# Blocks of 384 tokens in row groups of 128, a second product that yields rows, and a reciprocal held in PSUM, in an attention and two-mixture kernel

## The chip, the cores and the metric

The kernel runs on one NeuronCore of a Trainium2 chip. The metric is the device time in microseconds of one execution, as the median of several runs. Five engines work from queues of their own and meet through semaphores: PE (matrix products, results in PSUM), DVE and ACT (elementwise work, both reach SBUF and PSUM), POOL (elementwise work in SBUF and indirect DMAs) and SP (here it only issues DMAs).

## The reference

```python
# q, k, v: batch 8, heads 8, 576 tokens, head width 64
k_p = k.reshape(B, H, 72, 8, D).mean(axis=3)       # and v_p alike: 72 averaged keys
attn = softmax(q @ k_p.T / 8)                      # over the 72 keys
x = (attn @ v_p) as rows                           # 4608 tokens x 512
h = x @ w_in                                       # 512 x 2048, float64 in DRAM
g = (a0 + a1*h + a2*h*h + a3*h**3) / (1 + |b0|*|h| + |b1|*h*h + 1e-6)
y = g @ w_out                                      # 2048 x 512, float64 in DRAM
logits = y @ w_gate                                # 8 experts, the best one of each token
out = gate * (relu(y @ w1[e]) @ w2[e])             # 512 x 1024 x 512, float32
```

## The kernel before

Products are made in float32r from a high and a low part of each operand, so a product of two matrices is three products (high by high, high by low, low by high).

**Head.** `w_in` and `w_out` are turned from float64 into a high and a low float32r part, in 40 pieces (`conv_magnitude` on ACT, `conv_bits` and `conv_join` on DVE, `conv_high` on ACT, `conv_low` on POOL; line 281 `tick` does one stage of each for a different piece). 34 of the 40 ticks stand ahead of the first product, woven into the attention of the first block; the others stand in the first steps of the loop. The head ends with the first product at 109.4 us.

**Block loop.** A block is half a batch: 288 tokens, in three row groups of 96. It takes 16 steps, one for each chunk of 128 of the hidden width, so there are 16 blocks and 256 steps. Step t has, in this order of the code:

- `mm1(t)`: 12 products of 128x128 by 128x288, the hidden values of the chunk, by chunk on the partitions and token on the columns, into PSUM (`hps`, two buffers).
- `act_c(t - 2)`: Ln and Exp on ACT give the reciprocal of the denominator in SBUF (`Bt`), then two operations on DVE (lines 509 and 510) and later a third (512) finish the quotient with one step of Newton's.
- `act_d(t - 3)`: the quotient is split, the high part by ACT (518), the low part by POOL (519).
- `act_a(t)`, `act_b(t)`: numerator and denominator from `hps`, with ACT (484, 492, 499), DVE (493, 497) and POOL (500).
- `mm2(t - 4)`: 12 products of 128x128 by 128x288; the weights are the stationary operand, so the result `y` has the 512 output columns on the partitions, in four PSUM tiles, and the tokens on the columns.

`LAG`, here 4, is how many steps `mm2` is behind `mm1`. The attention of the next block is cut into events at points, two points to a step (`EVENTS`); one unit, a pair of heads of one block, takes 8 points, which is four steps. When a block is done, `evac` copies `y` to SBUF, `route1` and `route2` find expert and place of each token, and `rows` turns `y` back into rows with PE and writes them to DRAM (`yd`). Keys and values are pooled once for a batch, but the split of the values is made anew in each of its two blocks (`at_v`).

**Second mixture.** 17 full slots of 256 tokens and four half ones of one expert each: lists and rows are fetched by indirect DMAs, the expert's weights are loaded (512 KB pieces), split by ACT and DVE, and multiplied. The first three slots are known early and run while the last blocks are routed.

Nothing is scheduled by a planner: each engine takes its instructions in the order in which the code issues them.

Of the kernel before, what the change touches and what calls it, by code (L numbers as in the profile page):

```python
# [33 lines left out]
BUSY = 17      # slots of the full size that always run  # L34


def feasible(nt):
# [10 lines left out]
def const_layout(nt, nb):  # L48
    """Columns of the array of shape constants."""
    nth, nf, nr = nt // SL, BUSY - EARLY, n_rest(nt)  # L50
    cols, o = {}, 0
    for name, w in (("ident", 128), ("val", E), ("base", E), ("thr", 2 * nth), ("item", nf + nr + NU + nr),
                    ("place", nf + nr + NU + nr), ("low", E * E), ("eid", E), ("tok", nb * 6), ("mask", 2), ("vmask", 2)):
        cols[name] = (o, w)
        o += w
# [3 lines left out]
def constants(nt, nb):  # L59
# [19 lines left out]
    b, r = np.divmod(np.arange(nb * 6), 6)  # L79
    put("tok", b[None] * 576 + 6 * p[:, None] + r[None])  # L80
# [6 lines left out]
def tile_kernel(  # L87
# [24 lines left out]
    R = 3  # L112
    N = R * G
    NBLK = 2 * B
    LATE = 6
    ROW = DM + 1
    # the first units spare VectorE, which the weights hold
    LAG, WHOLE = 4, 4
# [8 lines left out]
    t3p = ctx.enter_context(tc.tile_pool(name="t3p", bufs=3))  # L127
    ysp = ctx.enter_context(tc.tile_pool(name="ysp", bufs=2))
# [5 lines left out]
    elp = ctx.enter_context(tc.tile_pool(name="elp", bufs=3))  # L134
    first = ExitStack()
    o1 = first.enter_context(tc.tile_pool(name="o1", bufs=1))
    kvl = first.enter_context(tc.tile_pool(name="kvl", bufs=4))
    t2p = first.enter_context(tc.tile_pool(name="t2p", bufs=2))
# [17 lines left out]
    ones = one.tile([G, 128], BF16, name="ones")  # L156
# [20 lines left out]
    tok = one.tile([G, 6 * B], I32, name="tok")  # L177
    nc.vector.tensor_copy(tok, con("tok")[:G])

# [8 lines left out]
    def clear_rows():  # L188
        zero = ysp.tile([G, ROW], F32, tag="ys", name="zero")
        nc.gpsimd.memset(zero, 0.0)  # L190
        nc.sync.dma_start(yd[(B - 1) * S:, :].rearrange("(p r) c -> p r c", r=2 * R),
                          zero.unsqueeze(1).to_broadcast([G, 2 * R, ROW]))
# [4 lines left out]
    def rest_parts(dtype, rows):  # L197
        t = [o1.tile([rows, w], dtype, tag=f"rest{w}", name=f"rest{w}") for w in (128, N)]
        for x in t:
            nc.vector.memset(f32(x), 0.0)  # L200
        return t

    tail = rest_parts(F32, KB)
# [16 lines left out]
    def conv_load(c):  # L220
        j, i, o, w = PIECES[c]
        if c == 0:
            sr = wp.tile([128, 4, 512], I64, tag="w", name="sr")
            mr = wp.tile([128, 8, 512], F32, tag="w", name="mr")
            cv["ring"] = [sr[:, x] for x in range(4)], [mr[:, x] for x in range(8)]
        if j < RING:
            s, m = cv["ring"][0][c % 4], cv["ring"][1][c % 8]
        else:
            s = kvl.tile([128, 256], I64, tag="kv", name="s64")
            m = None  # L230
# [7 lines left out]
        cv[c] = [s, m]  # L238

    def words(c):  # L240
        """The upper words of a piece, and its quarters."""
        s = cv[c][0]
        return s.bitcast(U32).rearrange("p (n t) -> p n t", t=2)[:, :, 1], s.bitcast(U16).rearrange("p (n t) -> p n t", t=4)

    def conv_magnitude(c):
        """The upper word of a float64, read as a float32 without its sign, times 2^-112: the
        exponent's upper bits are 0, and three places further on it is float32's."""
        if cv[c][1] is None:
            cv[c][1] = kvl.tile([128, 256], F32, tag="cm", name="m64", bufs=3)
# [785 lines left out]
```

## Time and profile before

| | us |
|---|---|
| median of 3 runs (1734.96 to 1739.96) | 1739.53 |
| span of the profiled execution, first to last instruction | 1722.4 |
| head, to the first product | 109.4 |
| block loop, to the first back product of the second mixture | 1133.6 |
| second mixture, to the last output DMA | 462.6 |
| what follows it in the span | 16.8 |
| busy in the span: PE / DVE / ACT / POOL | 1530.5 / 1464.8 / 1158.1 / 906.7 |

The profiled execution has a span of 1722.4 us; its own time outside of the span isn't recorded, and the median of the runs is 17.1 us above it. The shares over the whole span hide the stages: the loop and the second mixture have different limits, so the table is by stage. PE's busy time counts a modelled end of each product, so a product that nothing follows at once looks longer than the interval to the next in a dense row.

### The profile page before, as it was taken

How to read it: one execution, taken by the hardware profiler on the slowest of the kernel's cores; microseconds unless marked ns; L12 is line 12 of the kernel's file. 1: busy time of each engine (PE TensorE's matmuls, PEld its weight loads, DVE VectorE, ACT ScalarE, POOL GpSimd, SP SyncE). 2: the span in 40 equal slices, each digit the busy share in tenths (PEclk: the TensorE clock that was granted, in tenths of full speed). 3: DMA queues.
4: the chain of work that ended last, by engine and by line, in shares of the span. 5: the costliest groups of instructions: out<-in, count | busy, mean ns of one | idle time of the engine just before them, and what ended most of it. 6: DMA issues, size and time to landing. Idle time of an engine off the chain costs nothing. (4 is left out here: it accounts for less than half of the span.)

```text
span 1722.4 us, 31453 instructions
## 1 busy us (share of the span) xinstructions
PE 1530.5 (89%) x10920; PEld 1446.9 (84%) x10920; DVE 1464.8 (85%) x2986; ACT 1158.1 (67%) x2668; POOL 906.7 (53%) x1035
## 2 busy tenths in 40 slices
PE   0368999899999799989999989999879999999995
PEld 0248898898999799889899989999879998999994
DVE  7999999999999799999999999998866656666661
ACT  3467777777778578778677867877645556565651
POOL 6958756855856665675685676555412112112120
PEclk9998999999999899999999999999989999999998
DMA  6622211101201311110120120003667777777760
GB/s 202 191 86 59 50 35 32 43 21 44 49 8 44 40 26 42 32 39 18 44 49 13 48 46 15 19 13 71 175 154 248 237 231 240 246 237 246 239 202 18
DMA packets 144932, 165.72 MB, mean 96 GB/s; under 512 B 54206, under 2 KB 97470, under 8 KB 144768
## 3 DMA queue, kind: packets, MB, share of 16 engines
q1 hardware_dynamic: 137152, 144.21, 29.8%
q0 software_dynamic: 7616, 19.45, 3.4%
q8 instruction: 88, 1.44, 0.5%
q14 instruction: 76, 0.62, 0.2%
HBM read 143.37 MB, written 20.77 MB: 95 GB/s over the span
## 5 line engine op out<-in xcount | busy, mean ns | idle before, releaser
L530 PE MATMUL y<-hi,wt 128*128 128x288 f32 x2048 | 480.5, 309 | 25.1 <-DVE yT L542 25.1
L477 PE MATMUL hps<-xT,wt 128*128 128x288 f32 x3072 | 469.4, 302 | 7.6 <-DVE C L497 6.9
L477 PEld LDWEIGHTS hps<-xT,wt 128*128 128x128 f32 x3072 | 426.1, 191 | 13.8 <-DVE C L497 13.4
L530 PEld LDWEIGHTS y<-hi,wt 128*128 128x128 f32 x2048 | 351.1, 192 | 28.4 <-DVE yT L542 28.4
L519 POOL TENSOR_TENSOR lo<-C,hi 128x288 fp32r<-128x288 f32 x256 | 236.0, 922 | 212.8 <-ACT hi L518 148.4
L530 PE MATMUL y<-lo,wt 128*128 128x288 f32 x1024 | 309.3, 302 | 25.9 <-POOL lo L519 25.9
L814 DVE TENSOR_TENSOR wt<-ws,wt 128x1024 fp32r<-128x1024 f32 x168 | 203.2, 1222 | 100.2 <-ACT wt L809 99.3
L500 POOL TENSOR_TENSOR A<-A,B 128x288 f32<-128x288 f32 x256 | 235.2, 919 | 85.6 <-ACT B L499 65.4
L510 DVE SCALAR_TENSOR_TENSOR A<-A,qone,B 128x288 f32<-128x288 f32 x256 | 233.3, 911 | 0.0
L823 PEld LDWEIGHTS h2ps<-x2T,wt 128*128 128x128 f32 x1632 | 214.4, 192 | 20.7 <-DVE lo L836 9.4
L823 PE MATMUL h2ps<-x2T,wt 128*128 128x256 f32 x1632 | 219.0, 284 | 9.1 <-DVE lo L836 8.9
L518 ACT ACTIVATE hi<-C 128x288 fp32r<-128x288 f32 x256 | 112.2, 438 | 168.0 <-DVE C L512 166.3
L856 PE MATMUL o<-wt,hi 128*128 128x512 f32 x608 | 220.9, 405 | 1.3 <-ACT yT L540 0.8
L530 PEld LDWEIGHTS y<-lo,wt 128*128 128x128 f32 x1024 | 198.0, 193 | 28.2 <-POOL lo L519 28.0
L809 ACT ACTIVATE wt<-ws 128x1024 fp32r<-128x1024 f32 x168 | 174.8, 1055 | 16.5 <-PE o L856 16.5
L509 DVE SCALAR_TENSOR_TENSOR C<-C,ab,B 128x288 f32<-128x288 f32 x256 | 157.1, 614 | 20.6 <-ACT B L508 20.4
L499 ACT ACTIVATE B<-A,ab 128x288 f32<-128x288 f32 x256 | 160.0, 625 | 0.0
L512 DVE SCALAR_TENSOR_TENSOR C<-A,C 128x288 f32<-128x288 f32 x256 | 156.6, 612 | 0.1
L507 ACT ACTIVATE B<-A,qone 128x288 f32<-128x288 f32 x256 | 136.2, 532 | 22.5 <-POOL A L500 21.2
L492 ACT ACTIVATE C<-hps,ab 128x288 f32<-128x288 f32 x256 | 150.0, 586 | 1.2 <-POOL lo L519 1.2
L835 ACT ACTIVATE hi<-h2ps 128x256 fp32r<-128x256 f32 x136 | 52.0, 383 | 142.4 <-PE h2ps L823 140.2
L856 PEld LDWEIGHTS o<-wt,hi 128*128 128x128 f32 x608 | 115.0, 189 | 22.0 <-ACT yT L540 1.1
(277 smaller groups left out, 2684.6 us busy)
## 6 DMA issues: line engine op xcount, KB each, us to landing
ws<-in_moe_w_dram SPq DMA_DIRECT2D x168, 512.0 KB
yd<-ys SPq DMA_DIRECT2D x48, 192.4 KB
kt<-in_k_dram SPq DMA_DIRECT2D x64, 144.0 KB
qt<-in_q_dram SPq DMA_DIRECT2D x128, 72.0 KB
sr<-in_moe_w_in_dram SPq DMA_DIRECT2D x12, 512.0 KB
sr<-in_moe_w_out_dram SPq DMA_DIRECT2D x12, 512.0 KB
vt<-in_v_dram SPq DMA_DIRECT2D x32, 144.0 KB
vt<-in_v_dram SPq DMA_DIRECT2D x32, 112.0 KB
```

The source lines that it names most:

```text
L477: nc.tensor.matmul(hps, lhsT=w_in_part(t, wi, kk, fl), rhs=xT[n, kk][:, xi, :], start=(i == 0), stop=(i == last))
L499: nc.scalar.activation(Bt, A, AF.Identity, scale=b1, bias=b0)
L500: nc.gpsimd.tensor_tensor(out=A, in0=A, in1=Bt, op=ALU.mult)
L509: nc.vector.scalar_tensor_tensor(out=C, in0=C, scalar=a0, in1=Bt, op0=ALU.add, op1=ALU.mult)
L510: nc.vector.scalar_tensor_tensor(out=A, in0=A, scalar=qone, in1=Bt, op0=ALU.add, op1=ALU.mult)
L512: nc.vector.scalar_tensor_tensor(out=C, in0=A, scalar=-2.0, in1=C, op0=ALU.add, op1=ALU.mult)
L519: nc.gpsimd.tensor_tensor(out=lo, in0=C, in1=f32(hi), op=ALU.subtract)
L530: nc.tensor.matmul(yps[n][d], lhsT=w_out_part(w, wi, fl)[:, d * 128:d * 128 + 128], rhs=g[gi], start=(fc == 0 and i == 0), stop=(fc == NFC ...
L809: nc.scalar.activation(s["wt"][j][:, 2 * i, :], s["ld"][c], AF.Copy)
L814: nc.vector.tensor_tensor(out=t[:, 2 * i + 1, :], in0=w, in1=f32(t[:, 2 * i, :]), op=ALU.subtract)
L823: nc.tensor.matmul(hps, lhsT=a_, rhs=b_, start=(i == 0), stop=(i == 3 * KD - 1))
L856: nc.tensor.matmul(s["o"][j], lhsT=hl[gi][:, x * 128:(x + 1) * 128], rhs=w_out_part(wt_, wi, fl), start=(first_ and n_ == 0), stop=(last_ ...
```

## The change

Blocks become 384 tokens, two thirds of a batch, in three row groups of 128. Two batches make three blocks, so the middle block of each three has tokens of two batches (`pieces_of`), and there are 12 blocks and 192 steps. 576 is no multiple of 128, so one row group in nine is put together from two batches, 64 and 64 rows.

```diff
-G = 96         # tokens of one row group
+G = 128
+R = 3
...
+    pair, i = divmod(t, PER2)
+    a, whole = 2 * pair, HEADROWS // G
+    tail = SEQ - HEADROWS
+    if i < whole:
+        return [(0, G, a, i, whole)]
+    if i == whole:
+        return [(0, tail, a, HEADROWS, 1), (tail, G, a + 1, 0, 1)]
+    return [(0, G, a + 1, tail + i - whole - 1, whole)]
...
-    LAG, WHOLE = 4, 4
+    LAG = 3
...
-    t3p = ctx.enter_context(tc.tile_pool(name="t3p", bufs=3))
-    ysp = ctx.enter_context(tc.tile_pool(name="ysp", bufs=2))
+    t3p = ctx.enter_context(tc.tile_pool(name="t3p", bufs=2))
+    ysp = ctx.enter_context(tc.tile_pool(name="ysp", bufs=3))
...
     def conv_magnitude(c):
...
+        w = PIECES[c][3]
+        cv[c][1] = py.tile([128, 512], F32, tag=f"y{c % 3}", name="mag")[:, :w]
+        nc.scalar.activation(cv[c][1], words(c)[1].bitcast(F32), AF.Abs, scale=2.0 ** -112)
...
-        nc.gpsimd.tensor_tensor(out=wt[j][:, 2 * i + 1, o:o + w], in0=cv.pop(c)[1],
-                                in1=f32(wt[j][:, 2 * i, o:o + w]), op=ALU.subtract)
...
+        (nc.gpsimd if j < RING else nc.vector).tensor_tensor(
+            out=wt[j][:, 2 * i + 1, o:o + w], in0=cv.pop(c)[2], in1=f32(wt[j][:, 2 * i, o:o + w]), op=ALU.subtract)
...
+        parts = [kvp.tile([128, 2, D], F32R, tag=f"va{j}", name=f"va{j}") for j in range(2)]
+        nc.scalar.activation(parts[0], va, AF.Copy)
+        nc.gpsimd.tensor_tensor(out=parts[1], in0=va, in1=f32(parts[0]), op=ALU.subtract)
+        kv_t[bb, hp][1:] = [[x.rearrange("j h d -> j (h d)") for x in parts], end]
...
+            A, C = el[t]
+            Q = py.tile([128, N], F32, tag="y3", name="Q")
+            nc.scalar.activation(Q, A, AF.Ln, bias=qone)
+            nc.scalar.activation(Q, Q, AF.Exp, scale=-1.0)
+            nc.vector.scalar_tensor_tensor(out=C, in0=C, scalar=a0, in1=Q, op0=ALU.add, op1=ALU.mult)
+            nc.vector.scalar_tensor_tensor(out=Q, in0=A, scalar=qone, in1=Q, op0=ALU.add, op1=ALU.mult)
+            el[t] = Q, C
...
+            yps[n] = [py.tile([G, DM], F32, tag=f"y{r}", name=f"y{r}") for r in range(R)]
...
+        for r in range(R):
+            for i, (wi, gi) in enumerate(((0, 0), (1, 0), (0, 1))):
+                nc.tensor.matmul(yps[n][r], lhsT=g[gi][:, r * G:(r + 1) * G], rhs=w_out_part(w, wi, fl),
+                                 start=(fc == 0 and i == 0), stop=(fc == NFC - 1 and i == 2))
...
+    def evac(n):
+        rows_t[n] = []
+        for r in range(R):
+            ys = ysp.tile([G, DM], F32, tag="ys", name="ys")
...
+            for lo, hi, dst in places(n * R + r):
+                nc.sync.dma_start(dst[:, :DM], ys[lo:hi])
...
-    P0, PACE, HEAD = 8, 1.55, 34      # the weights that are made ready before the first product
+    P0, PACE, HEAD = 6, 1.2, 39
...
-            p2["stg"] = ctx.enter_context(tc.tile_pool(name="stg", bufs=5))
+            p2["stg"] = ctx.enter_context(tc.tile_pool(name="stg", bufs=4))
...
-            act_c(t - 2, 0)
-        if 3 <= t < total + 3:
-            act_d(t - 3)
+            act_d(t - 2)
+        if 1 <= t < total + 1:
+            act_c(t - 1, 0)
```

In `mm2` the quotient is now the stationary operand and the weights move: 9 products of 128x128 by 128x512, whose result has tokens on the partitions. `evac` copies these rows and writes them to `yd` at once; for the routing each row group is turned by PE (`logits`), copied, and multiplied by `w_gate` (`logits2`). The gates follow in DMAs of one column (`gates`). The split values of a pair of heads are made once for a batch and kept. `y` needs three PSUM tiles instead of four; the fourth holds the reciprocal `Q`. 39 ticks instead of 34 stand ahead of the first product, and the quotient is finished one step earlier (`act_c(t - 1)`, `act_d(t - 2)`).

The order of the engines' instructions, in the middle of the loop, before and after. First **DVE**, one step and the start of the next. `C` is the numerator and then the quotient, `A` the denominator, `B` (now `Q`) the reciprocal, `hps` the hidden values in PSUM; equal numbers are the same tile.

```order
L509 SCALAR_TENSOR_TENSOR C_6547<-C_6547,ab_111,B_6552 128x288
L510 SCALAR_TENSOR_TENSOR A_6539<-A_6539,qone_116,B_6552 128x288
L493 TENSOR_TENSOR C_6669<-C_6669,hps_6640 128x288
L512 SCALAR_TENSOR_TENSOR C_6547<-A_6539,C_6547 128x288
L497 SCALAR_TENSOR_TENSOR C_6669<-C_6669,ab_111,hps_6640 128x288
```

The same place in the changed kernel:

```order
L555 SCALAR_TENSOR_TENSOR C_4850<-C_4850,ab_111,Q_4886 128x384
L556 SCALAR_TENSOR_TENSOR Q_4886<-A_4844,qone_116,Q_4886 128x384
L538 TENSOR_TENSOR C_4899<-C_4899,hps_4869 128x384
L560 SCALAR_TENSOR_TENSOR C_4850<-Q_4886,C_4850 128x384
L542 SCALAR_TENSOR_TENSOR C_4899<-C_4899,ab_111,hps_4869 128x384
```

The five operations keep their order; `Q` stands in PSUM where `B` and the product in `A` stood in SBUF, and the quotient that is finished belongs to the step just before instead of the one before that.

Then **ACT**, from the Ln of one step to that of the next. `hi` is the high part of the quotient; L507 and L508, now L553 and L554, are Ln and Exp.

```order
L507 ACTIVATE B_7583<-A_7566,qone_116 128x288
L508 ACTIVATE B_7583<-B_7583 128x288
L518 ACTIVATE hi_7695<-C_7513 128x288
L484 ACTIVATE A_7699<-hps_7678 128x288
L361 ACTIVATE qT_7705<-qps_7701 128x288
L492 ACTIVATE C_7715<-hps_7678,ab_111 128x288
L499 ACTIVATE B_7720<-A_7699,ab_111 128x288
L445 ACTIVATE xT_7740<-ops_7735 128x288
L507 ACTIVATE B_7657<-A_7636,qone_116 128x288
```

The changed kernel, from the last operation of a step to the last of the next:

```order
L544 ACTIVATE Bt_5597<-A_5569,ab_111 128x384
L566 ACTIVATE hi_5628<-C_5512 128x384
L553 ACTIVATE Q_5632<-A_5569,qone_116 128x384
L554 ACTIVATE Q_5632<-Q_5632 128x384
L529 ACTIVATE A_5637<-hps_5615 128x384
L410 ACTIVATE qT_5643<-qps_5639 128x384
L537 ACTIVATE C_5653<-hps_5615,ab_111 128x384
L544 ACTIVATE Bt_5658<-A_5637,ab_111 128x384
```

Before, Ln takes an `A` from two steps back (7566; the step's own is 7699). Now Ln takes the `A` (5569) that belongs to the L544 two rows above it, with POOL's product of the two in between, and `hi` moved ahead of Ln.

Last **PE**, the first product of a step and the start of its second. `pps` and `sps` are parts of the attention of the next block, `y` the result of the block.

```order
L477 MATMUL hps<-xT,wt 128x288 x12
L398 MATMUL pps<-cst,pt 16x96 x3
L530 MATMUL y_5039<-hi,wt 128x288
L530 MATMUL y_5039<-lo,wt 128x288
L530 MATMUL y_5039<-hi,wt 128x288
L530 MATMUL y_5040<-hi,wt 128x288
```

The changed kernel, with the outputs of a unit (`ops`) between:

```order
L419 MATMUL sps<-kbd,qT 128x144 x3
L522 MATMUL hps<-xT,wt 128x384 x12
L489 MATMUL ops<-pT_4920,va_3871 128x384
L489 MATMUL ops<-pT_4921,va_3871 128x384
L489 MATMUL ops<-pT_4920,va_3872 128x384
L489 MATMUL ops<-tail,end_132 128x384
L578 MATMUL y_4112<-wt,hi 128x512 x2
L578 MATMUL y_4112<-wt,lo 128x512
L578 MATMUL y_4113<-wt,hi 128x512 x2
```

In each step 24 products of 288 columns became 12 of 384 and 9 of 512, and the first of the low part moved from second to third in `mm2`.

## Rows read from the trace of the kernel before

**Rows 1.** Windows: stretch, length, busy us of PE, PEld, DVE, ACT, POOL; clock.

```profile
0.00:109.40 109.40, 31.03 (x105) 19.37 (x105) 96.95 (x145) 45.01 (x93) 81.93 (x69) 1.00 0.56 174
109.40:1243.00 1133.60, 1048.15 (x7905) 1018.86 (x7903) 1084.46 (x2368) 853.09 (x2139) 733.74 (x888) 0.98 0.18 41
1243.00:1705.60 462.60, 451.27 (x2914) 408.69 (x2914) 283.38 (x475) 260.01 (x438) 90.35 (x78) 0.99 0.69 216
1705.60:1722.40 16.80, 0.00 (x0) 0.00 (x0) 0.00 (x0) 0.00 (x0) 0.65 (x1) 0.54 0.03 11
```

**Rows 2.** DVE by line, 300 to 1100 us: busy us, mean ns, idle before.

```profile
L510 DVE SCALAR_TENSOR_TENSOR A<-A,qone,B 128x288 f32<-128x288 f32 x181 | 166.5, 920 | 0.0
L512 DVE SCALAR_TENSOR_TENSOR C<-A,C 128x288 f32<-128x288 f32 x182 | 111.0, 610 | 0.0
L509 DVE SCALAR_TENSOR_TENSOR C<-C,ab,B 128x288 f32<-128x288 f32 x182 | 108.9, 598 | 18.2 <-ACT B L508 18.1
L497 DVE SCALAR_TENSOR_TENSOR C<-C,ab,hps 128x288 f32<-128x288 f32 x182 | 91.4, 502 | 0.0
L493 DVE TENSOR_TENSOR C<-C,hps 128x288 f32<-128x288 f32 x182 | 79.6, 437 | 0.7
L331 DVE TENSOR_REDUCE kp<-kt 72x64 f32<-72x512 f32 x45 | 48.3, 1073 | 0.7
...
L374 DVE TENSOR_TENSOR pt<-sps,mx 96x432 f32<-96x432 f32 x46 | 27.8, 604 | 1.6
```

**Rows 3.** A line's instructions, 300 to 1100 us: duration ns min/median/max.

```profile
L497 DVE SCALAR_TENSOR_TENSOR C<-C,ab,hps x182: 495/502/510, 300.5 to 1099.0; 128x288 f32<-128x288 f32 x182
...
L510 DVE SCALAR_TENSOR_TENSOR A<-A,qone,B x181: 500/1057/1936, 303.0 to 1096.6; 128x288 f32<-128x288 f32 x181
```

**Rows 4.** Timeline of DVE and POOL at one place: start, length.

```profile
505.82 1.23 DVE L510 SCALAR_TENSOR_TENSOR A<-A,qone,B 128x288 f32<-128x288 f32 x1
505.90 0.82 POOL L519 TENSOR_TENSOR lo<-C,hi 128x288 fp32r<-128x288 f32 x1
```

**Rows 5.** POOL, the same view.

```profile
L500 POOL TENSOR_TENSOR A<-A,B 128x288 f32<-128x288 f32 x183 | 168.2, 919 | 55.9 <-ACT B L499 42.7 <-PE y L530 7.8
```

**Rows 6.** PE timeline in the block loop: start, length, count.

```profile
501.07 1.75 PE L477 MATMUL hps<-xT,wt 128*128 128x288 f32 x12
502.65 0.41 PE L359 MATMUL qps<-cst,qt 96*128 96x96 f32 x3
...
509.15 0.98 PE L368 MATMUL sps<-kbd,qT 128*96 128x144 f32 x6
```

**Rows 7.** PE timeline in the second mixture.

```profile
1503.03 0.39 PE L856 MATMUL o<-wt,hi 128*128 128x512 f32 x1
...
1504.42 1.59 PE L823 MATMUL h2ps<-x2T,wt 128*128 128x256 f32 x12
```

**Rows 8.** PE, by line and shape, 300 to 1100 us.

```profile
L552 PE MATMUL tps<-wg,yT 128*96 128x8 f32 x264 | 23.4, 227 | 0.0
```

**Rows 9.** ACT by line, 300 to 1100 us, columns as in group 2.

```profile
L507 ACT ACTIVATE B<-A,qone 128x288 f32<-128x288 f32 x182 | 96.9, 532 | 22.2 <-POOL A L500 21.2
L508 ACT ACTIVATE B<-B 128x288 f32<-128x288 f32 x182 | 81.0, 445 | 5.8
L518 ACT ACTIVATE hi<-C 128x288 fp32r<-128x288 f32 x182 | 79.8, 438 | 121.0 <-DVE C L512 120.5
...
L616 ACT ACTIVATE ys<-rp 96x512 f32<-96x512 f32 x36 | 21.1, 587 | 0.0
```

**Rows 10.** DVE by line and shape, 0 to 109.4 us.

```profile
L257 DVE TENSOR_SCALAR sr<-sr 128x512 uint16<-128x512 uint16 x24 | 28.6, 1191 | 0.0
...
L262 DVE SCALAR_TENSOR_TENSOR mr<-mr,sr 128x512 uint32<-128x512 uint32 x24 | 21.0, 875 | 0.2
```

**Rows 11.** PE timeline where routing ends.

```profile
1283.55 2.93 PE L823 MATMUL h2ps<-x2T,wt 128*128 128x256 f32 x12 [8.94 <-DVE lo L836]
```

**Rows 12.** Waits, 1180 to 1320 us: total, times, longest.

```profile
ACT ys L616 <- DMA yd<-ys: 9.4, 1, 9.4
```

More of the change, by code (lines that the diff above doesn't have):

```diff
@@ L24 @@
 SL = 256
-G = 96
+G = 128
+R = 3
+HEADROWS = 512
 POOL = 8
@@ L78, in constants @@
     put("eid", np.arange(E))
-    b, r = np.divmod(np.arange(nb * 6), 6)
-    put("tok", b[None] * 576 + 6 * p[:, None] + r[None])
+    tok = np.zeros((128, nt // G))
+    for t in range(nt // G):
+        for lo, hi, batch, start, step in pieces_of(t):
+            tok[lo:hi, t] = batch * SEQ + start + step * np.arange(hi - lo)
+    put("tok", tok)
     put("mask", np.stack([p < 64, p >= 64], 1))
@@ L188, in clear_rows @@
     def clear_rows():
-        zero = ysp.tile([G, ROW], F32, tag="ys", name="zero")
+        zero = ysp.tile([96, ROW], F32, tag="ys", name="zero")
         nc.gpsimd.memset(zero, 0.0)
-        nc.sync.dma_start(yd[(B - 1) * S:, :].rearrange("(p r) c -> p r c", r=2 * R),
-                          zero.unsqueeze(1).to_broadcast([G, 2 * R, ROW]))
+        nc.sync.dma_start(yd[(B - 1) * S:, :].rearrange("(p r) c -> p r c", p=96),
+                          zero.unsqueeze(1).to_broadcast([96, S // 96, ROW]))
     KB = 2 * KP - 128
[L197 to L203, printed above, removed]
+    tail = o1.tile([64 + KB, N], F32R, name="tail")
+    nc.vector.memset(f32(tail), 0.0)
+    ends = [o1.tile([64 + KB, 128], F32R, name=f"end{i}") for i in range(HP + 1)]
+    for x in ends:
+        nc.gpsimd.memset(f32(x), 0.0)
     wt, cv = {}, {}
@@ L222, in conv_load @@
         if c == 0:
[L223 to L230, printed above, removed]
+            cv["ring"] = []
+            for x in range(2):
+                ring = wp.tile([128, 4, 512], I64, tag="w", name="sr")
+                cv["ring"] += [ring[:, y] for y in range(4)]
+        s = cv["ring"][c % 8] if j < RING else ysp.tile([128, 256], I64, tag="ys", name="s64")
         if i == 0:
@@ L298, in unit, with runs @@
         n, hp = divmod(U, HP)
-        return n, hp, *divmod(n, 2)
+        a, m = 2 * (n // 3), n % 3
+        return n, hp, a, (a, a + 1, None)[m]
+    def runs(n):
+        out_ = []
+        for r in range(R):
+            for lo, hi, batch, _, _ in pieces_of(n * R + r):
+                if out_ and out_[-1][2] == batch:
+                    out_[-1][1] = r * G + hi
+                else:
+                    out_.append([r * G + lo, r * G + hi, batch])
+        return out_
     def at_load_kv(U, h):
-        n, hp, bb, half = unit(U)
-        if half == 0:
+        n, hp, _, bb = unit(U)
+        if bb is not None:
             kt = kvl.tile([128, POOL * D], F32, tag="kv", name="kt")
@@ L342, in at_kT @@
     def at_kT(U):
-        n, hp, bb, half = unit(U)
-        if half == 0:
-            kp = kv_t[hp][0]
+        n, hp, _, bb = unit(U)
+        if bb is not None:
+            kp = kv_t[bb, hp][0]
             kps = pm.tile([128, KP], F32, tag="m", name="kps")
@@ L397, in at_pT @@
         for r in range(R):
[L398 removed]
+            nc.tensor.transpose(pps[:, r, :], pt[:, r, 128:] if h else pt[:, r, :128], ident)
         pps = pps.rearrange("j r g -> j (r g)")
         if h == 0:
[L401 removed]
+            parts = [o1.tile([128, N], F32R, tag=f"pT{j}", name=f"pT{j}") for j in range(2)]
@@ new lines, in tile_kernel, with places @@
+    rows_t, lg_t = {}, {}
+    def evac(n):
+        rows_t[n] = []
+        for r in range(R):
+            ys = ysp.tile([G, DM], F32, tag="ys", name="ys")
+            if r == 1:
+                nc.vector.tensor_copy(ys, yps[n][r])
+            else:
+                nc.scalar.activation(ys, yps[n][r], AF.Copy)
+            rows_t[n].append(ys)
+            for lo, hi, dst in places(n * R + r):
+                nc.sync.dma_start(dst[:, :DM], ys[lo:hi])
+    def places(t):
+        out_ = []
+        for lo, hi, batch, start, step in pieces_of(t):
+            at = batch * S + start
+            if step > 1:
+                first_ = start if batch % 2 == 0 else start - (SEQ - HEADROWS)
+                rows_ = yd[at - first_:at - first_ + step * G, :].rearrange("(p r) c -> p r c", r=step)[:, first_, :]
+            else:
+                rows_ = yd[at:at + hi - lo, :]
+            out_.append((lo, hi, rows_))
+        return out_
@@ L595, in route2 @@
         if n == NBLK - 3:
-            soon = early_tables()
-            for i in range(5):
-                agenda.setdefault(p + 2 + 2 * i, []).append((lambda: next(soon, None), None))
+            agenda.setdefault(p + 2, []).append((lambda: list(early_tables()), None))
         for r in range(R):
@@ L625, in after_block @@
             todo += [(p + 4, lambda _: next(tables, None))] * LATE
-        at, gap = {NBLK - 2: (p + 9, 3), NBLK - 1: (p + 5, 3)}.get(n, (p + 4, 1))
-        todo += [(at + gap * r, lambda _, r=r: rows(n, r)) for r in range(R)]
         return todo
@@ L995, in tile_kernel @@
                 evac(n)
-                extra += after_block(n, 2 * t + LEAD + (4 if n < NBLK - 2 else 3))
+                extra += after_block(n, 2 * t + LEAD + 2)
         main.back(g)
```

248 lines of the change are left out of this document (124 added, 124 removed).

## The prediction

> **What bounds the kernel now.** I read the windows by stage first, since the shares over the span mix stages with different limits. In the block loop DVE is busy for 1084.5 of 1133.6 us, 96%, and PE, by its modelled ends, for 1048.2, 92%; ACT has 75% and POOL 65% [rows 1]. Over 256 steps that is 4.43 us a step, of which DVE works 4.24. In the second mixture PE is busy for 451 of 462.6 us and nothing else is near it. In the head DVE is busy for 97 of 109.4 us. So DVE sets the pace of head and loop, PE that of the rest.
>
> Next I asked what fills DVE in the loop. The list of its instructions by line shows five operations of every step, 920, 610, 598, 502 and 437 ns on 288 columns, 3.07 us together [rows 2]. The two that read `hps` in PSUM keep their length: 495 to 510 ns for one line. The three that read two tiles in SBUF don't: the same work takes 500 to 1936 ns, in the median 1057 [rows 3]. The timeline shows when: one of them took 1.23 us beside a POOL product of 0.82 us that began with it [rows 4]. POOL makes two such products a step, 919 ns in the mean [rows 5]. So some 0.7 us of DVE's step (920, 610 and 598 down to about 500, 440 and 500) is waiting for POOL.
>
> **The change, part by part.**
>
> *Reciprocal in PSUM.* The three slow operations keep one operand in SBUF; the other, and in one case the result, moves to PSUM. The nearest row for that is the 502 ns line with its 495 to 510 [rows 3]. It shows no wait for POOL and no extra for the PSUM operand either, since the SBUF form has the same 500 ns when alone. I take those lengths; the bound on the other side is that nothing gets shorter. [...]
>
> *384 columns.* From 288 to 432 columns a DVE operation goes from 437 to 604 ns [rows 2], about 1.1 ns a column, so 96 more columns cost 0.1 us and the fixed part is paid 192 times, not 256. The five come to 500+500+440+502+437 = 2.38 us plus 0.53 for columns, 2.9 a step; neighbours overlap by some 0.05 each, which leaves 2.65. DVE's other work is now 4.24 - 3.07 + 0.25 = 1.4 us a step, 363 us in all; 48 units instead of 64, with a third more columns in part of their operations, and the split of the values made half as often and partly by POOL, leave some 80%, 290 us or 1.5 a step. DVE: 4.15 us a step, 800 us, far below the loop of now.
>
> *Second product turned.* PE's dense intervals are 1.58 us for 12 products of 288 columns (501.07 to 502.65) [rows 6], 132 ns each, and 1.39 us for 6 of 512 (1503.03 to 1504.42) [rows 7], 232 ns each; between them lies 175 ns for 384. A step goes from 24 x 132 = 3.16 us to 12 x 175 + 9 x 232 = 4.18. Over the loop this is 809 before and 803 after: the columns are the same, only the fixed part of 2112 products goes. The rest of PE's 1048 us busy, 239 us, is attention, routing and modelled ends. Three quarters of it, for 48 units and 12 blocks, is 179 us, 0.93 a step. From below: a unit needs 0.98 us for its scores [rows 6], four products of 132 ns, and a quarter of the 2.1 us of small products of a block (23.4 us for 11 blocks) [rows 8], 2.0 us for four steps, 0.5 a step, without any transpose. PE then needs 4.7 to 5.1 us a step and is the engine with most to do.
>
> *Copies and rows.* A block's 12 transposes and small products remain, in another place; so do its copies: four of 288 columns and three row copies of 512 (587 ns [rows 9]) before, three and three of 512 now, 1152 columns less and 1536 more. I cost the difference at nothing; what hides it is DVE's 0.9 us free in a step. Without that cover 384 columns at 1.1 ns come to 0.4 us a block, 5 us. SP has more to issue: in the middle block of three a unit's queries come in eight DMAs instead of two, and row groups of two batches need two writes for rows and for gates. The gates wait in SP's queue for DVE's routing, and the loads of the units behind them; those stand three steps ahead (queries) and seven (keys and values), some 15 us and more, which covers it.
>
> *Shorter pipeline and fewer buffers.* `Q` and `Bt` have one buffer, hi and lo two, the quotient is due a step earlier. In ACT's order Ln now waits for the POOL product of the step just before. POOL takes 0.81 us alone for 288 columns by the timeline [rows 4], so 1.1 for 384; ACT has a copy (hi, 438 ns now [rows 9]) in that time, so about 0.6 us of ACT is open each step, and ACT, at 853 us now, comes to some 720, 3.7 a step. Behind Ln stand Exp, then all of DVE's work on `Q`. This fits a step of 5.1 but not with much to spare (first rival).
>
> *Head.* DVE gains five pieces of 256 columns (two shifts at half of the 1191 ns [rows 10], a join and a subtraction near 0.4: 2.0 us each), five poolings of 1.07 us [rows 2], eight subtractions of 0.54, and eight more subtractions of 0.4 that POOL made before: 23 us. It loses 24 x 0.18 us at the join, which no longer reads two SBUF tiles (875 ns [rows 10] to about 690), 4.4 us. 109.4 + 18.6 would be 128; some of DVE's 12 idle us may fill, so 126. Nothing hides it: DVE is the head's bound. The loop loses five ticks for it, some 10 us of DVE that PE's pace covers.
>
> *Second mixture.* Its products are unchanged. With two buffers, hi of a step can be written only when the back product of two steps earlier is done; the next front product covers that. The loads have four buffers instead of five, and the list of waits there names none for a load. One stall of 8.94 us [rows 11] stands before it gets going: ACT waits 9.4 us for a `ys` buffer whose DMA is late [rows 12]. These row writes leave ACT's queue in the second mixture, so I take 462.6 - 9.6 = 453.
>
> **Sum**, against the profiled span of 1722.4 us. I take 5.15 us a step: PE's upper figure and a little for block ends and the clock (0.98 granted [rows 1]). Head 126; loop 192 x 5.15 = 989; three remaining second products, two front products and a last wait 14; second mixture 453; end 16.8 [rows 1]. That is 1599, and 17 more to the median of the runs as before: 1616 us, 123 us or 7% less.
>
> **Rivals.**
>
> *ACT and DVE pace the loop.* The ring hi, Ln, Exp, three operations on `Q`, an attention operation between, and back to hi: 0.52 + 0.62 + 0.53 + 0.6 + 0.6 + 0.9 + 0.54 + 0.55 = 4.9 us with the lengths scaled to 384 columns (ACT's copies go from 445 to 587 ns between 288 and 512 columns [rows 9], which gives 0.06 for 96 more, plain proportion 0.15; I take 0.09), and 5.45 with hops and a POOL product that comes late behind pooling. For it: DVE waited only 18 us for Exp [rows 2], now that slack is a step shorter. Against: the queues have some slack in most steps. 192 x 0.3 = 58 more: 1674. [...]
>
> *PE at its floor.* If attention and routing cost nearer the lower figure, 4.9 a step, and the head comes to 118: 1616 - 48 - 8 = 1560. For it: 239 us contains modelled ends. Against: while DVE sets the pace, PE shows no more than 8% idle [rows 1], so some of its waits hide in the busy time of both.
>
> *PSUM doesn't free DVE.* Then 0.7 us a step stays, a third longer: DVE works 5.05 and the step is 5.3: 1645. Against: the 495 to 510 ns.
>
> *Slower.* ACT and POOL in lockstep: hi, Ln, Exp, Abs and the two affine operations 3.5 us, an attention copy 0.6, POOL's product 1.1, and whatever POOL does ahead of it in its own order (up to 0.9 for the normalisation of a unit), 6.1 us when nothing overlaps: 192 x 0.95 = 182 more, 1798. It decides from 5.8 us a step on. Against: POOL's other work is spread over four steps, and ACT's first copy lies in its shadow.
>
> **Numbers.** Forecast (1590 to 1645 us) 0.55; ACT and DVE ring 0.2; PE floor 0.12; PSUM without effect 0.05; slower 0.05, the remaining 0.03 near no change. The range takes in the floor and most of the ring: 1565 to 1680. Faster by over 0.3% 0.93, within 0.3% 0.02, slower 0.05; 0.3% is about what a measurement of this kernel can tell from no change.
>
> **What would show it.** L556 at about 0.6 us with a narrow minimum to maximum; DVE busy near 80 to 85% of the loop and PE above 94%; first product at 120 to 135 us; no wait of 9 us near the end of routing. I am wrong if ACT's Ln waits for POOL in most steps, if PE waits for lo or `hps` for more than 0.3 us a step, or if the second mixture gets longer than 460 us.

## The result

The changed kernel takes 1666.6 us in the median of four runs (1661.61 to 1668.18); the kernel before took 1738.2 us beside it. The ratio is 0.959 (95% interval 0.956 to 0.962): 71.6 us or 4.1% faster. I had forecast faster, and 1616 us; 1666.6 lies inside the range of 1565 to 1680, near the price of the first rival (1674). It lies outside the 1590 to 1645 to which I gave 0.55.

By stage, with the stretches cut as in [rows 1] (first product of the first mixture, last second product, last product of all), the windows of the changed kernel read: length, then busy us of PE, PEld, DVE, ACT and POOL, granted clock, DMA share, GB/s.

```profile
0.00:118.60 118.60, 27.08 (x93) 17.99 (x94) 103.55 (x187) 51.67 (x109) 71.17 (x89) 1.00 0.59 182
118.60:1181.10 1062.50, 997.97 (x5430) 879.94 (x5430) 820.13 (x1716) 734.68 (x1520) 587.20 (x721) 0.99 0.19 39
1181.10:1650.90 469.80, 455.10 (x2926) 410.44 (x2926) 289.16 (x481) 258.38 (x440) 91.19 (x74) 0.99 0.71 217
1650.90:1666.30 15.40, 0.00 (x0) 0.00 (x0) 0.00 (x0) 0.00 (x0) 0.98 (x1) 0.58 0.03 12
```

By these two profiles the whole gain is in the loop, 1133.6 to 1062.5 us; head and second mixture are 9.2 and 7.2 us longer. (Their spans differ by 56.1 us, not by 71.6: that of the kernel before was quicker than its median, and no profile shows where the other 15 us lie.) DVE, 96% busy in the loop before, is at 77%. PE is at 94%. 192 steps take 5.53 us each; the forecast had 5.15, or 5.22 with its 14 us for the end of the loop, which this window holds.

The operations on the reciprocal now have fixed lengths. Three lines' instructions, in ns as in [rows 3], and the DVE lines from 200 to 1100 us, as in [rows 2]:

```profile
L555 DVE SCALAR_TENSOR_TENSOR C<-C,ab,Q x192: 596/615/618, 129.5 to 1172.9; 128x384 f32<-128x384 f32 x192
...
L556 DVE SCALAR_TENSOR_TENSOR Q<-A,qone,Q x192: 607/617/619, 130.0 to 1173.5; 128x384 f32<-128x384 f32 x192
...
L560 DVE SCALAR_TENSOR_TENSOR C<-Q,C x192: 539/551/557, 131.7 to 1174.1; 128x384 f32<-128x384 f32 x192
```

```profile
L556 DVE SCALAR_TENSOR_TENSOR Q<-A,qone,Q 128x384 f32<-128x384 f32 x162 | 99.9, 617 | 0.0
L555 DVE SCALAR_TENSOR_TENSOR C<-C,ab,Q 128x384 f32<-128x384 f32 x161 | 98.8, 614 | 152.9 <-ACT Q L554 152.9
L542 DVE SCALAR_TENSOR_TENSOR C<-C,ab,hps 128x384 f32<-128x384 f32 x162 | 97.9, 604 | 0.0
L560 DVE SCALAR_TENSOR_TENSOR C<-Q,C 128x384 f32<-128x384 f32 x162 | 89.1, 550 | 0.0
L538 DVE TENSOR_TENSOR C<-C,hps 128x384 f32<-128x384 f32 x162 | 88.6, 547 | 19.8 <-ACT C L537 17.5
```

The operation that took 500 to 1936 ns before takes 607 to 619 on a third more columns. DVE now waits 152.9 us for Exp in these 900 us; before it waited 18.2 us in the 800 of [rows 2].

The list of waits, 200 to 1100 us (us in total, times, longest), shows a loop without one ruler: engines wait for each other in a ring.

```profile
POOL A L545 <- ACT Bt L544: 251.9, 127, 4.7
DVE C L555 <- ACT Q L554: 152.9, 113, 8.5
ACT hi L566 <- DVE C L560: 125.1, 104, 3.8
ACT Q L553 <- POOL A L545: 54.3, 33, 7.3
...
POOL kt L389 <- issue: 35.4, 6, 7.3
...
PE y L578 <- POOL lo L567: 13.4, 7, 3.5
```

The line with "issue" is the one to follow: a pause of POOL that the profile ascribes to nothing. The timelines of POOL, ACT and PE at one of its six places (start, length, and in brackets the idle time before and its releaser):

```profile
369.58 1.03 POOL L681 DMA_INDIRECT ids<-tok,pi  x1 [0.17 <-issue]
370.68 1.01 POOL L567 TENSOR_TENSOR lo<-C,hi 128x384 fp32r<-128x384 f32 x1
377.84 1.27 POOL L389 TENSOR_TENSOR kt<-kt 16x256 f32<-16x256 f32 x2 [6.16 <-issue]
```

```profile
380.61 0.58 ACT L553 ACTIVATE Q<-A,qone 128x384 f32<-128x384 f32 x1 [6.15 <-POOL A L545]
```

```profile
381.58 0.50 PE L578 MATMUL y<-wt,lo 128*128 128x512 f32 x1 [2.37 <-POOL lo L567]
...
386.35 0.52 PE L449 MATMUL pps<-cst,pt 128*128 128x128 f32 x3 [2.91 <-DVE kbd L399]
```

POOL issues a write of the token lists (an indirect DMA), then one product, and then stands still ahead of the pooling of the last 16 value rows. ACT's Ln waits 6.15 us for POOL's next product, and PE pays 2.37 and 2.91 us. In the order of the program that pooling waits for the list write: the third of its waits below is the write's semaphore.

```
272 L681 DMA ids<-tok,pi 37120x1 [waits DMASW3_49]
273 L567 TENSOR_TENSOR lo<-C,hi 128x384 [waits PE_49,Activation_49,Pool_49]
274 L389 TENSOR_TENSOR kt<-kt 16x256 [waits DMAHW0_49,DMAHW6_49,DMASW4_49,Pool_49]
```

A list write needs 8.4 us in the median to land (200 to 1100 us). By the trace this one lands at 377.72, and POOL goes on at 377.84; at all six places it goes on 0.12 to 0.13 us behind the landing of the write just ahead of it. The pooling reads nothing of the lists.

### The profile page after: what moved, and what is told of

It reads as the page before. It is cut to its first block, busy times and chain, and to the rows that moved or that the text cites. A ratio compares the mean times of both kernels' runs of the same rounds, so it can differ in the third digit from the quotient of the medians.

```text
span 1666.3 us, 25442 instructions
## 1 busy us (share of the span) xinstructions
PE 1480.1 (89%) x8448; PEld 1308.4 (79%) x8448; DVE 1212.8 (73%) x2382; ACT 1044.7 (63%) x2068; POOL 750.5 (45%) x885
## 5 line engine op out<-in xcount | busy, mean ns | idle before, releaser
L522 PE MATMUL hps<-xT,wt 128*128 128x384 f32 x2304 | 452.9, 345 | 1.7 <-DVE C L542 1.7
L578 PE MATMUL y<-wt,hi 128*128 128x512 f32 x1152 | 371.8, 404 | 1.8 <-DVE wt L295 1.8
L545 POOL TENSOR_TENSOR A<-A,Bt 128x384 f32<-128x384 f32 x192 | 194.2, 1011 | 302.4 <-ACT Bt L544 300.0
L555 DVE SCALAR_TENSOR_TENSOR C<-C,ab,Q 128x384 f32<-128x384 f32 x192 | 117.8, 614 | 174.5 <-ACT Q L554 174.1
L578 PE MATMUL y<-wt,lo 128*128 128x512 f32 x576 | 229.3, 398 | 13.9 <-POOL lo L567 13.9
L578 PEld LDWEIGHTS y<-wt,hi 128*128 128x128 f32 x1152 | 207.5, 190 | 36.6 <-DVE wt L295 2.1
L567 POOL TENSOR_TENSOR lo<-C,hi 128x384 fp32r<-128x384 f32 x192 | 195.3, 1017 | 58.6 <-ACT hi L566 49.8
L553 ACT ACTIVATE Q<-A,qone 128x384 f32<-128x384 f32 x192 | 110.6, 576 | 59.9 <-POOL A L545 58.6
L578 PEld LDWEIGHTS y<-wt,lo 128*128 128x128 f32 x576 | 109.1, 189 | 41.8 <-POOL lo L567 17.5
L544 ACT ACTIVATE Bt<-A,ab 128x384 f32<-128x384 f32 x192 | 135.7, 707 | 3.1 <-DVE ti L754 3.1
L537 ACT ACTIVATE C<-hps,ab 128x384 f32<-128x384 f32 x192 | 127.9, 666 | 0.0
```

The lines of the kernel that those rows point to most:

```text
L522: nc.tensor.matmul(hps, lhsT=w_in_part(t, wi, kk, fl), rhs=xT[n, kk][:, xi, :], start=(i == 0), stop=(i == last))
L537: nc.scalar.activation(C, hps, AF.Identity, scale=a3, bias=a2)
L544: nc.scalar.activation(Bt, A, AF.Identity, scale=b1, bias=b0)
L545: nc.gpsimd.tensor_tensor(out=A, in0=A, in1=Bt, op=ALU.mult)
L553: nc.scalar.activation(Q, A, AF.Ln, bias=qone)
L555: nc.vector.scalar_tensor_tensor(out=C, in0=C, scalar=a0, in1=Q, op0=ALU.add, op1=ALU.mult)
```

## The experiments

Ratios are to the kernel before on the same chip, with their 95% intervals. "Loop" runs, as above, from the first product of the first mixture to the end of the last second product, read from each profile.

| kernel | us | ratio | loop us | a step | PE busy of it |
|---|---|---|---|---|---|
| before | 1738.2 | 1 | 1133 | 4.42 | 1048 |
| changed | 1666.6 | 0.959 (0.956 to 0.962) | 1062 | 5.53 | 998 |
| q_sbuf | 1738.9 | 1.003 (1.002 to 1.004) | 1137 | 5.92 | 1023 |
| before_tp | 1740.1 | 1.004 (1.002 to 1.005) | 1155 | 4.51 | 1130 |
| pe_less | 1625.7 | 0.938 (0.936 to 0.941) | 1022 | 5.32 | 893 |
| ring_less | 1722.7 | 0.993 (0.991 to 0.996) | 1024 | 5.33 | 987 |
| both_less | 1668.4 | a single run | 966 | 5.03 | 875 |
| scatter_late | 1625.5 | 0.939 (0.937 to 0.941) | 1022 | 5.32 | 988 |
| hi_after | 1660.8 | 0.959 (0.956 to 0.961) | 1061 | 5.53 | 1001 |
| quot_early | 1649.3 | 0.953 (0.950 to 0.955) | 1045 | 5.44 | 993 |
| scatter_quot | 1608.7 | 0.928 (0.926 to 0.931) | 1001 | 5.21 | 981 |
| best | 1627.0 | 0.939 (0.937 to 0.941) | 1025 | 5.34 | 993 |
| before_late | 1705.3 | 0.985 (0.983 to 0.987) | 1112 | 4.34 | 1042 |
| late_pe_less | 1591.3 | 0.919 (0.917 to 0.921) | 985 | 5.13 | 875 |

**The parts of the change.** First the reciprocal alone, put back into SBUF.

```diff
-            Q = py.tile([128, N], F32, tag="y3", name="Q")
+            Q = elp.tile([128, N], F32, tag="Q", name="Q", bufs=1)
```

> The changed kernel with the reciprocal back in SBUF (a tile of its own; small tiles of the keys and the routing give up their second buffer for the room). Theory A, the PSUM tile is what frees DVE from POOL: the three operations that use it go from 614, 617 and 550 ns to about 1000, 1100 and 750 in the mean, with maxima above 1.8 us; DVE gets 1 us more to do in a step and the chain Ln, Exp, DVE, hi is longer by as much, so a step goes from 5.53 to 5.9 to 6.2 us: 1740 to 1800 us. Rival B, the place of the tile does not matter: within 10 us of 1667.

```profile
L555 DVE SCALAR_TENSOR_TENSOR C<-C,ab,Q x192: 590/619/3192, 128.4 to 1246.3; 128x384 f32<-128x384 f32 x192
L556 DVE SCALAR_TENSOR_TENSOR Q<-A,qone,Q x192: 617/619/1271, 129.1 to 1247.0; 128x384 f32<-128x384 f32 x192
L560 DVE SCALAR_TENSOR_TENSOR C<-Q,C x192: 537/936/2835, 130.8 to 1247.7; 128x384 f32<-128x384 f32 x192
```

Theory A holds: the three lines in min/median/max are long again, up to 3.2 us, the step is 5.92 us, and the kernel is no faster than before. Two of my means were too high and the third too low (704, 650 and 821 ns from 200 to 1200 us, not 1000, 1100 and 750). The edit also takes the second buffer from five small tiles; over the whole loop the three lines cost 0.42 us a step more, 81 us, and the loop is 75 us longer, so they are enough to explain it.

Then the other side: the kernel before with the second product turned and the reciprocal in PSUM, still in blocks of 288 tokens (the copies and logits by rows, as in the changed kernel, come with it).

```diff
-                nc.tensor.matmul(yps[n][d], lhsT=w_out_part(w, wi, fl)[:, d * 128:d * 128 + 128], rhs=g[gi],
+                nc.tensor.matmul(yps[n][r], lhsT=g[gi][:, r * G:(r + 1) * G], rhs=w_out_part(w, wi, fl),
```

> The kernel before (288 columns, 256 steps) with two parts of the change alone: the second product turned (96 rows of 512 columns, nine products instead of twelve of 288) and the reciprocal in the PSUM bank that this frees. Theory A: DVE is freed of 0.7 us a step, but PE gets 9 x 232 - 12 x 132 = 0.50 us more to do, since 96 rows fill only three quarters of the array; PE then paces the loop at 4.65 to 4.9 us a step instead of 4.43: 1790 to 1860 us, slower than before. Rival B: DVE paced so firmly that its relief wins: under 1735.

It is slower than before, by 0.4%, not by the 3 to 7% I had put down. In the loop PE is busy for 1130 of 1155 us, 98%, DVE for 942, 82%: the relief of DVE is there, and PE takes all of it. With 96 rows instead of 128 the products aren't shorter: six of 144 columns for the scores take 0.90 us with 96 rows (before, at 317.61 us) and with 128 (changed, at 322.10). My step was too long since PE's other work is shorter than its busy time before had made it look: 4.41 busy less 12 x 132 + 9 x 232 = 3.67 leaves 0.74 us a step, where 239 us over 256 steps [rows 1] had been 0.93.

So neither part gains without the other. The turn frees the PSUM tile for the reciprocal; blocks of 384 make the turn free for PE.

**What sets 5.53 us.** PE lightened, the ring of ACT and DVE lightened, and both:

```diff
-            for i, (wi, gi) in enumerate(((0, 0), (1, 0), (0, 1))):
+            for i, (wi, gi) in enumerate(((0, 0), (0, 1))):
```

> The changed kernel without the products of the high part of the activation with the low part of the weights in the second product (three of nine of 512 columns; the output is then less exact). It takes 0.70 us of PE out of each step, and nothing from any other engine. Theory A, PE paces the loop: most of 192 x 0.70 = 134 us goes, to 1535 to 1570 us. Rival B, the ring of ACT and DVE (hi, Ln, Exp, three operations) or that of ACT and POOL paces it: under 25 us go, 1640 to 1667.

```diff
-            nc.vector.scalar_tensor_tensor(out=C, in0=C, scalar=a0, in1=Q, op0=ALU.add, op1=ALU.mult)
+            nc.vector.scalar_tensor_tensor(out=C[:, :h], in0=C[:, :h], scalar=a0, in1=Q[:, :h], op0=ALU.add, op1=ALU.mult)
```

(and the operation that follows it, with `Q` for its result, in the same way; `h` is 192.)

> The changed kernel with two of the three DVE operations on the reciprocal done on 192 of 384 columns (the output is then wrong in half of the columns). The chain hi, Ln, Exp, DVE, hi gets 0.4 us shorter in each step, and DVE has 0.4 us less to do; PE's work is as before. Theory A, PE paces the loop and waits for single late steps only: 0 to 15 us less, 1650 to 1667. Rival B, the ring of ACT and DVE paces it: 192 x 0.4 = 77 us less, about 1590.

> The two lightened kernels in one: three of nine products left out of the second product, and two DVE operations on half of the columns (output wrong, and with it the routing and the second mixture, so only the loop is read). Theory A, PE and the ring of ACT and DVE hold the loop back together, each near 5.3 us a step: with both lightened a step goes to 4.8 to 5.0 us, the loop to 930 to 960 us. Rival B, a third thing, POOL's order or ACT's, stands at 5.3 already: the loop stays above 1000 us.

Each theory gets a part. pe_less leaves out 576 products of 232 ns, 134 us; PE's busy time falls by 105, the loop loses 41, and PE idles for 129. Without 0.4 us of the ring the loop loses 38 of 77, and PE's idle time falls from 64 to 38. With both it loses 97, to 966, a little above what theory A of both_less gave. (ring_less sends tokens to other experts: its second mixture takes 575 us instead of 469, which is why its total is high; only its loop is read.) With either lightened a step is 5.32 or 5.33 us, with both 5.03: neither sets the 5.53 alone, and what comes late on either is paid.

PE's granted clock has a part in these runs. The traces show two levels, 1.00 and 0.50 of full speed, and it stands at the lower one for 20 us of the loop in the changed kernel and for 72 in pe_less. Two windows of the changed kernel, in the form of [rows 1], the first from the start of POOL's standstill:

```profile
372.00:387.00 15.00, 9.73 (x51) 8.21 (x51) 6.76 (x13) 5.20 (x12) 6.60 (x9) 1.00 0.10 25
387.00:390.40 3.40, 3.40 (x13) 3.21 (x12) 3.24 (x6) 3.07 (x9) 2.68 (x5) 0.50 0.01 3
```

PE works for 9.7 of 15 us, and then the clock falls to 0.50. At that level 12 products of 128x256 take 2.93 us (at 1238.61 us, where the clock is 0.50; shown below), at the upper one 1.59 [rows 7]; there, from 1503 to 1506 us of the kernel before, it is 1.00. So 52 us more at the lower level cost pe_less up to 26 us, an estimate; its gain of 41 understates what PE's work is worth.

**POOL's pause.** The second and third list write of a block are recorded later, behind the poolings.

```diff
-            agenda.setdefault(p + 1 + (4 if n < NBLK - 1 else 3) * r, [])...
+            agenda.setdefault(p + ((1, 7, 15)[r] if n < NBLK - 3 else 1 + (4 if n < NBLK - 1 else 3) * r), [])...
```

> The changed kernel with the second and third list write of a block (the indirect DMAs of POOL) recorded some points later, behind the small poolings of the values instead of just ahead of them. In the changed kernel POOL stands still for 4.4 to 7.3 us, six times, right behind such a write, and PE then waits 2.4 to 6 us for lo and for the normalised scores. Theory A, this standstill is a wait for the list write to land and PE pays for it: POOL's standstills go, PE's idle time of 63 us in the loop falls by 20 to 30 us, the time by as much, to 1635 to 1648. Rival B, POOL's pause is not tied to the write, or the ring of ACT and DVE takes up the time anyway: within 5 us of 1667.

All six pauses are gone, the loop is 41 us shorter, PE's idle time 31 us and its busy time 10. The time is 0.939 of before, against 0.959. PE's waits for lo (13.9 us in the loop) and for `kbd`, a tile of the pooled keys (14.6), are down to 0.5 us. Four of the six pauses had been followed by the lower clock level (at 387, 565, 653 and 831 us); the loop now has 10 us of it instead of 20, which by the same estimate is 5 us of the busy time. The same edit on the kernel before:

> The kernel before with its list writes moved behind the poolings in the same way. POOL stands still there too (3.2 to 8.9 us behind a list write, one unit in two blocks), and PE waits 26 us for lo in the loop. Theory A, the standstill is older than the change and costs the kernel before about as much: 20 to 35 us less, 0.98 to 0.99. Rival B, the longer pipeline of the kernel before (lo is used four steps later, not three, and hi and lo have three buffers) covers it, and it is the change that made it cost something: under 8 us less, 0.995 to 1.

1.5%, 27 us (2.1% on the changed kernel): the pause is older than the change, and rival B, that the longer pipeline covers it, falls. With it gone on both sides the change is worth 0.939/0.985 = 0.953.

**The ring.** Two ways to shorten it by order alone. ACT's copy to hi behind Ln and Exp:

```diff
+        if 1 <= t < total + 1:
+            act_c(t - 1, 0)
         if 2 <= t < total + 2:
             act_d(t - 2)
-        if 1 <= t < total + 1:
-            act_c(t - 1, 0)
```

> The changed kernel with one thing in another order: ACT copies hi of a step after Ln and Exp of the next step, not ahead of them. With one buffer for Q, Ln must wait for the last DVE operation on Q; hi (523 ns) no longer stands between the two, so the ring Ln, Exp, three DVE operations is shorter by some 0.5 us a step, and nothing else is. Theory A, the ring holds a good part of the steps back: the loop gets 20 to 50 us shorter, as with the three operations on half of the columns (38 us), to 1617 to 1647. Rival B, that run gained because DVE had less to do: within 5 us of 1667. Rival C, lo comes a microsecond later and PE waits for it: over 1670.

No gain that can be told. PE now waits 18.3 us for ACT's hi, six times, each within 10 us of the end of one of POOL's pauses, and 19 for the tail (14 in the changed kernel); its waits for lo and `kbd`, 13.9 and 14.6 us there, are down to 1.7. One wait behind the pauses took the place of another, and the lower clock level takes 41 us of the loop, not 20. What this order is worth without the pauses no run shows. And the last operation on `Q` at once behind the one before:

```diff
             act_c(t - 1, 0)
+            act_c(t - 1, 1)
...
-            act_c(t - 1, 1)
```

> The changed kernel with the last DVE operation on Q recorded directly behind the one before it, not after an attention operation and the first of the numerator. Theory A, the ring through the one buffer of Q holds the steps back: it gets shorter by 0.5 us and by the attention operation that lies between in half of the steps, so 20 to 50 us go, to 1617 to 1647. Rival B, the numerator of the next step is late instead and the PSUM tile of the first product with it, or the operations do not follow each other without a gap: 1660 to 1690.

0.953: the loop loses 17 us, a little less than theory A's 20, and the time lies between the two ranges. Together with the late list writes:

> The changed kernel with both orders that gained: the list writes behind the poolings, and the last DVE operation on Q directly behind the one before it. Theory A, with POOL's standstills gone PE is busy for 97% of the loop (1021 us), and a shorter ring can only take what is left of PE's idle time, 32 us, of which 15 are waits for the tail's copy: 0 to 15 us less than with the list writes alone, 0.930 to 0.939 of the time before. Rival B, the two gains add up, 17 us from the ring whatever else waits: 0.925 to 0.930.

0.928 (0.926 to 0.931): nearer to the sum of the two, and the fastest kernel of the study, 1608.7 us. The windows of its loop and two lines of its waits, 200 to 1080 us, show what is left:

```profile
117.58:1118.16 1000.58, 980.51 (x5430) 876.53 (x5430) 840.39 (x1716) 743.67 (x1520) 587.30 (x721) 1.00 0.22 42
```

```profile
DVE C L555 <- ACT Q L554: 89.4, 82, 2.1
...
ACT hi L566 <- DVE C L560: 11.6, 29, 1.0
```

The second of them in scatter_late, in the same stretch:

```profile
ACT hi L566 <- DVE C L560: 127.4, 108, 3.8
```

ACT's wait for the quotient, 127.4 us with late list writes alone, is 11.6, and PE is busy for 98%. In its place Ln waits for POOL's product, 85.9 us in 134 of the 192 steps of the loop, against 20.5 us in 32. Of the 21 us that the loop loses, 14 are idle time of PE and 7 its busy time, for the same 5430 products. In scatter_late, with PE busy for 97%, the ring still held PE back. late_pe_less says the same:

> The changed kernel with the list writes behind the poolings and without three of the nine products of the second product (less exact): PE has 0.70 us less to do in a step. Theory A, with the standstills gone PE alone paces the loop: more goes than the 41 us that this edit took from the changed kernel, and the loop falls from 1021 to between 900 and 960 us. Rival B, the ring of ACT and DVE stands close behind at 5.1 to 5.2 us a step: the loop stays between 975 and 1000.

The loop is 985.4 us, 5.13 a step, PE idle for 110 of it. Rival B: even without POOL's pause the ring stands right behind PE.

**A move that cost.** The copy of the probabilities' tail from POOL to DVE, on top of scatter_quot.

```diff
-        nc.gpsimd.tensor_copy(tail[64:], f32(tail[:KB]))
+        nc.vector.tensor_copy(tail[64:], f32(tail[:KB]))
```

> The same as the kernel with both orders, and the copy of the tail of the probabilities from one part of its tile to another moved from POOL to DVE. PE waits 15 us for that copy in the loop, because it stands in POOL's order behind the products. Theory A: 8 to 15 us go beside the kernel without this move. Rival B, the DVE operation takes as long as the wait (its queue is 80% full): within 4 us of it.

18 us slower than without it. DVE's timeline, and POOL's at the second place:

```profile
452.17 0.35 DVE L462 CAST tail<-tail 16x384 fp32r<-16x384 f32 x1
470.15 0.97 DVE L462 CAST tail<-tail 16x384 fp32r<-16x384 f32 x1
```

```profile
469.88 1.02 POOL L567 TENSOR_TENSOR lo<-C,hi 128x384 fp32r<-128x384 f32 x1
```

The copy takes 0.35 us where POOL has nothing running. Beside a POOL product that ends at 470.90, 0.75 us after the copy's start, it takes 0.97: that wait and some 0.2. It stands in DVE's queue, in the ring; PE's waits for it (7.2 us), for the logits (5.6) and for routing (7.9) rose. PE's idle time is 11 us longer in the loop and its busy time 13, and the lower clock level takes 31 us instead of 3: up to 14 us by the estimate above, so about half of the loss may be the clock's.

## Why the prediction was right, and where it was wrong

**Right: the parts.** *Reciprocal in PSUM* said 2.9 us for the five operations; they take 614 + 617 + 550 + 604 + 547 ns = 2.93. DVE comes to 4.27 us a step (820 us), forecast 4.15. The shortest of the same operations in SBUF are 590, 617 and 537 ns (q_sbuf), the shortest of the PSUM forms 596, 607 and 539, and their medians 615, 617 and 551: by the shortest, none is over 6 ns longer from PSUM. That PSUM frees DVE is shown by q_sbuf, 1.003 against 0.959. *Second product turned* is nearly right: PE is busy for 5.20 us a step, 5.11 in the fastest kernel, forecast 4.7 to 5.1.

**Wrong: the step of 5.15 us.** The sum took PE's upper figure "and a little for block ends and the clock". That little was 0.04 us; it measured 0.42, 5.53 against the 5.11 that PE is busy in the fastest kernel. By the runs, 0.21 is the pause behind the list writes (1062 to 1022 us), and 0.11 the order of the last operation on `Q`, which makes the ring nearly as long as PE's work (1022 to 1001). The remaining 0.1 is routing, logits and copies at block ends, and modelled ends; PE waits 4.7 us for `ys` copies and 3.5 for routing in the changed kernel, which I had at nothing. The pause could have been read in the trace before. Its waits from 200 to 1100 us have POOL's wait for "issue", and I passed it by as idle time of an engine at 65% that nothing waited for:

```profile
POOL kt L339 <- issue: 26.5, 6, 8.9
```

POOL's products are links of the ring, so its standstill is everybody's.

**The rival.** *ACT and DVE pace the loop* gave 1674 us by 0.3 us a step. That the time is near is partly luck, since the mechanism is half of it: lightening the ring alone gives back 38 us, lightening PE alone 41. One engine's own work doesn't give the step where a second chain is as long within 5%.

**Head: 118.6 us, forecast 126.** DVE works 103.6 us there, not 115.6. The terms too large were the shifts (963 and 988 ns against 1008 and 1191 in the head of before: 6 us for 24 of each; POOL has less beside them, 71 us against 82, but no run shows that this is why) and the joins of the small pieces, which I left at their old 881 ns and which take 416 (4 us).

**Second mixture: 469.8 us, forecast 453.** I took out the stall of 8.94 us [rows 11, 12] with the row writes, which I read as its cause. A stall of 7.39 us stands in nearly the same place. The list of waits there, 1120 to 1260 us, SP's own from 1150, and PE's timeline:

```profile
ACT wt L883 <- DMA ws<-in_moe_w_dram: 19.1, 6, 7.9
```

```profile
SPq L835 <- DMA ids<-tok,pi: 9.5, 1, 9.5
```

```profile
1238.61 2.93 PE L897 MATMUL h2ps<-x2T,wt 128*128 128x256 f32 x12 [7.39 <-DVE lo L910]
```

ACT waits for a load of weights, and DVE and PE wait for ACT in turn. SP's queue holds the load of a slot's list, which waits 9.5 us for the last list write, with more weights behind it. It is not what ACT waited for, by SP's issues and ACT's timeline:

```profile
1204.68 19.63 SPq L875 DMA_DIRECT2D ws<-in_moe_w_dram  x8
1234.63 0.37 SPq L835 DMA_DIRECT2D idi<-ids  x1
1235.88 6.41 SPq L875 DMA_DIRECT2D ws<-in_moe_w_dram  x5
```

```profile
1235.90 1.06 ACT L883 ACTIVATE wt<-ws 128x1024 fp32r<-128x1024 f32 x1 [7.94 <-DMA ws<-in_moe_w_dram]
```

By its semaphore, the load for which ACT waits is one of the eight: it was issued at 1218.38 and landed at 1235.88, just as the next was issued. Why it took 17.5 us stays open. In pe_less, where SP waits for no list write, the stall is 7.8 us, in late_pe_less 8.8; in q_sbuf, scatter_late, hi_after, quot_early, scatter_quot and best it is 3.0 to 5.5. So the step that failed is that the stall would go with the row writes. The change also has four load buffers instead of five, which I took to cost nothing; before_tp, with five and with its rows out of ACT's queue, stalls for 3.2 us at most and takes 459 us there. No run gave the buffer back. The stall is 7.4 of the 16.8 us; PE's busy time is 3.8 longer (12 more products fall behind the end of the loop, 1.6 us), and the rest is short waits.

**Seventeen microseconds of offset.** I added to the span what lay between span and median before. In the four runs of the changed kernel a run's time is 1.8 us above its span; so some 15 of the 17 must have been a quick profiled execution of the kernel before.

In numbers, against the forecast: head -7.4, loop +59.5 (1062.5 against 989 and 14), second mixture +16.8, end -1.4, offset -16.7: +50.8, and 1616 becomes 1667. Head and offset hid 24 us of what loop and second mixture cost; that is luck. Of the signs of being wrong that I had named, the second mixture above 460 us came true; Ln waits for POOL in 39 of 192 steps, and PE for lo and `hps` for 0.08 us a step.

## What to carry to other kernels

An engine with much idle time can still be a link in the chain that sets the pace: follow each long pause of it, one marked "issue" above all, to what waits behind it, and look in the recorded order for what the paused instruction waits on. When a change relieves the busiest engine, price the next one with the waits between engines, not by its busy time alone: here two chains came out within 5% of each other and the step lay 8% above both. Read the granted clock beside every kernel that is lightened to find its limit, since an engine that idles more can lose at a lower clock a part of what it gained (pe_less: 72 us of the loop at half the clock, against 20). Parts of a change can be worth nothing singly and 4% together when one part frees what another needs, here a PSUM tile.

## What the runs showed of the hardware

In best, DVE's copy of the tail, with a single SBUF input, was longer beside a running POOL product, as the two-input operation of [rows 4] was: 0.35 us alone, 0.97 beside one. Of its 48 copies (350 to 1827 ns, 590 in the median), five began with POOL free and took 0.35 us; 42 began beside a POOL operation and ended 0.21 to 0.22 us behind it, whatever was left of it (0.35 to 0.97 us). In the copy shown it is 0.75 us until POOL's end and 0.2 after. The row's shape alone, one input, doesn't tell: the sums of the pooled keys (L381 in the changed kernel), with one SBUF input too, take 995 to 1103 ns in all 64, with POOL free or running when they began.

ACT was quicker to PSUM: Ln takes 570 ns and Exp 475 in the changed kernel, 602 and 525 with `Q` in SBUF (q_sbuf; medians; Exp reads its source from the same place). That is 32 and 50 ns less for 384 columns.

POOL's list writes take 8.4 us in the median to land (5.2 to 9.6, changed kernel, 200 to 1100 us), and one POOL instruction that touches no list waits for them by the program's own semaphores. It is one on rows that begin at partition 96. Why it gets that wait is open; no run placed those rows elsewhere.
